# A transformer block on one core: from 128-row contractions and a planner to 64-row pairs and a written order

## The chip, the cores and the metric

The kernel runs on one core of a Trainium2 chip. The metric is the device time of one execution in microseconds (us); of the kernel before there are three timed runs, and their median is used.

## The reference

One block with adaptive layer norm: the vector `c` gives six modulation rows, the tokens go through a dilated sliding-window attention and then through an MLP. S = 2048 tokens, D = 448, 16 heads of 28, F = 1792, everything in bf16.

```python
mod = (_silu(c) @ w_mod).reshape(c.shape[0], 6, 1, -1)
sa, ca, ga, sb, cb, gb = ...
h = _layernorm(x) * (1 + ca) + sa
x = x + ga * _A_ref(h, A_wqkv, A_wo)
h = _layernorm(x) * (1 + cb) + sb
x = x + gb * _B_ref(h, B_w1, B_b1, B_w2, B_b2)

def _A_ref(x, wqkv, wo):          # 16 heads, window of 8 keys, every second token
    q, k, v = ...                 # x @ wqkv
    idx = pos[:, None] - 2 * jnp.arange(8)[None, :]
    logits = einsum('bhsd,bhswd->bhsw', q, k[idx]) * 28 ** -0.5   # masked where idx < 0
    o = einsum('bhsw,bhswd->bhsd', softmax(logits), v[idx])
    return o @ wo

def _B_ref(x, w1, b1, w2, b2):    # a second layer norm inside
    return gelu(_layernorm(x) @ w1 + b1) @ w2 + b2
```

A token attends to itself and to seven earlier tokens of its own parity, so even and odd tokens never meet in the attention.

## The kernel before

**Layout.** Even and odd tokens are two sequences of 1024, laid one behind the other along the free dimension. `x_all` holds 16 blocks of 128 tokens (eight of each parity). Transposed activations (`hT`, `qT`, `kT`, `oT`) have features or heads on the partitions and tokens along the free dimension. D = 448 is contracted in four steps of 128, 128, 128 and 64 or 65 rows (`KT`, `KW`, `KE`; the 65th row carries a bias or a zero), always on the whole array of TensorE (PE).

**Front.** `front_ln` takes the layer norm of two or four blocks (`stats`, `rstd_act` or `rstd_pool`, `normalize`), transposes on PE into `ptr` and applies scale and shift in `evac_h`. `front_qk` makes queries and keys, `pq`, with the weights spread to 32 rows per head by `spread`, in units of 256 (twice) and 512 (three times) columns: eight outputs m of four matmuls each, 160 matmuls in all. `mod_cols` makes the scale and shift columns from `silu_bf`; `mods` makes the other four modulation rows `pb`, stores them to `mod_hbm` and loads them back on all partitions (`mod_bc`). Behind that load, in the same SP queue, come the MLP weights (`load_mlp`).

**Attention.** Nine blocks, each of two sub-blocks of 114 queries in two windows. `values` copies the 64 key columns of two overlapping windows to `hw` and makes `pv` in four matmuls of 448 columns. `lmm` makes logits `lt` with keys on the partitions, in 32x64 tiles; ACT takes exp, DVE multiplies by `mask`. `dmm` makes the denominators `pd` with a matrix of ones and the outputs `po`, with heads on the partitions, in 64x32 tiles. ACT takes Ln and Exp of `pd` to get the reciprocals `lden`, and DVE's `div` multiplies into `oT`.

**After it.** `out_proj` makes `pw` from four head groups (`wo_s`, padded to 32 rows per head), adds it to `x_all`, takes both layer norms, and sends the result `ybuf` through a transposing DMA to `yT`. `x1p` on POOL keeps x plus the scaled bias of the MLP. `mlp` works on 256 tokens: per output tile of w1, four matmuls of 256 columns (`p1`), gelu on ACT into `hm`, then w2 with 14 matmuls of 448 columns per 128 tokens (`p2`), the residual on DVE and the store.

**Order.** Each piece is a task with an engine, an estimated time, reads, writes and buffers. `Planner.plan` runs a list schedule many times with perturbed ranks, keeps the best, and `emit` writes the program in that order, with filler matmuls (`pwm`) at the start. Each engine runs its instructions in the order written. PSUM has two large buffers (`L`, two banks) and four small ones (`S`, one bank).

The loop at the end of the kernel gives the phases: attention blocks 0 to 2, MLP tile 0; blocks 3 and 4, tiles 1 and 2; blocks 5 and 6, tiles 3 and 4; blocks 7 and 8, tiles 5 to 7.

Of the kernel before, what the change touches and what calls it, by code (L numbers as in the profile page):

```python
# [11 lines left out]
FP32 = mybir.dt.float32  # L12
# [5 lines left out]
DP = 512  # L18
KT, KR = 4, 64
KW = (128, 128, 128, KR)  # L20
KE = (128, 128, 128, KR + 1)
HP = 32
FT = F // 128
WIN = 8
SL = 1024
LEAD, SEP = 8, 8
WQ, WK, WE = 57, 64, 58
SBQ, NSB, NBT = 2 * WQ, 18, 9
SBE = 4 * WE
WT = LEAD + SL + SEP + SL + 4  # L30
OTW = NSB * SBQ
NBLK = S // 128
EPS = 1e-5
DEN_SCALE = 2.0 ** -32
EXP_SET = "natural_log_exp_and_others"
START, NOISE, WINDOW = 0.8, 0.02, 3.4133
SEED, TURNS = 44, 60
QKE = "AAADAAAD"
BONUS = (0.0, 0.0, 0.0)
SPREAD = (("DVE", "DVE"), ("DVE", "DVE"))  # L40
PHASES = [
    (range(0, 3), [0]),
    (range(3, 5), [1, 2]),
    (range(5, 7), [3, 4]),
    (range(7, 9), [5, 6, 7]),
]
LMM, DMM = 0.55, 0.80
FILL_UNTIL, FILL_SHARE = 12.0, 1.0
ROOM = {"L": 2, "S": 4, "et": 2, "den": 2, "zh": 6, "yT": 3, "hm": 3, "vb": 4, "hw": 3}
SWITCH, SAME = 0.095, 1.0  # L50
SEM = 0.07
DRAIN = {"PE": 0.165, "DVE": 0.085, "ACT": 0.105, "POOL": 0.05, "SP": 0.0}


class Buf:


    def __init__(self, room, make, name=""):
        self.room, self.make, self.name, self.users, self._t = room, make, name, [], None
        self.slot = None  # L60
# [8 lines left out]
class Task:  # L69
    def __init__(self, n, eng, us, fn, bufs, rank_add, late, dense, port, mode):  # L70
        self.n, self.eng, self.us, self.fn, self.bufs = n, eng, us, fn, bufs
        self.name = f"{eng} {fn.__qualname__.split('.')[-1]}:{fn.__code__.co_firstlineno}"
        self.rank_add, self.late, self.dense, self.port, self.mode = rank_add, late, dense, port, mode
        self.before, self.after = {}, []
        self.rank = 0.0
        self.fill = 0


class Planner:

    def __init__(self):
        self.tasks, self.writer, self.readers = [], {}, {}

    def add(self, eng, us, fn, reads=(), writes=(), bufs=(), after=(), order_after=(), rank_add=0.0, late=0.0, dense=1.0, port=False, mode="F"):
        t = Task(len(self.tasks), eng, us, fn, bufs, rank_add, late, dense, port or eng == "POOL", mode)
        for k in list(reads) + [b for b in bufs]:
            if k in self.writer:
                self._edge(self.writer[k], t, True)  # L90
        for k in writes:
            if k in self.writer:
                self._edge(self.writer[k], t, True)
            for r in self.readers.get(k, ()):
                self._edge(r, t, True)
            self.writer[k], self.readers[k] = t, []
        for k in reads:
            self.readers.setdefault(k, []).append(t)
        for b in bufs:
            b.users.append(t)  # L100
        for a in after:
            self._edge(a, t, True)
        for a in order_after:
            self._edge(a, t, False)
        self.tasks.append(t)
        return t

    def wrote(self, task, *bufs):
        for b in bufs:
            self.writer[b] = task  # L110

    def _edge(self, a, b, full):
        if a is b:
            return
        if a not in b.before:
            a.after.append(b)
            b.before[a] = full
        else:
            b.before[a] = b.before[a] or full

    def ranks(self):
        for t in reversed(self.tasks):
            tail = 0.0
            for a in t.after:
                lag = (DRAIN[t.eng] + SEM + t.late) if a.before[t] else 0.0
                tail = max(tail, a.rank + lag)
            t.rank = t.us + tail + t.rank_add

    def backward(self):

        used = {e: [] for e in DRAIN}
        for t in sorted(self.tasks, key=lambda t: (-(t.start + t.us), -t.n)):
            tail = 0.0
            for a in t.after:
                same = a.eng == t.eng and (t.eng == "PE" or not a.before[t])
                lag = 0.0 if same or not a.before[t] else DRAIN[t.eng] + SEM + t.late
                tail = max(tail, a.rank + lag)
            spans = used[t.eng]
            k = bisect.bisect_left(spans, (tail, 0.0))
            if k > 0 and spans[k - 1][1] > tail:  # L140
                tail = spans[k - 1][1]
            while k < len(spans) and spans[k][0] < tail + t.us - 1e-9:
                tail = max(tail, spans[k][1])
                k += 1
            t.rank = tail + t.us
            spans.insert(k, (tail, t.rank))

    def forward(self):
        left = {t: len(t.before) for t in self.tasks}
        ready_at = {t: 0.0 for t in self.tasks}  # L150
        ready = {e: [] for e in DRAIN}
        for t in self.tasks:
            if left[t] == 0:
                ready[t.eng].append(t)
        room = {r: [0.0] * n for r, n in ROOM.items()}
        users_left = {b: len(b.users) for t in self.tasks for b in t.bufs}
        free_at = {e: START for e in DRAIN}
        order = []
        now = START
        mode = "F"  # L160
        port = {"DVE": 0.0, "POOL": 0.0}
        while len(order) < len(self.tasks):
            started = False
            for e in ("PE", "DVE", "ACT", "POOL", "SP"):
                if free_at[e] > now:
                    continue
                best, best_key = None, None
                shared = e in port and port["DVE" if e == "POOL" else "POOL"] > now
                for t in ready[e]:
                    if ready_at[t] > now or (shared and t.port):  # L170
                        continue
                    key = (t.rank + (SAME if e == "PE" and t.mode == mode else 0.0), -t.n)
                    if best is not None and key < best_key:
                        continue
                    need = {}
                    for b in t.bufs:
                        if b.slot is None:
                            need[b.room] = need.get(b.room, 0) + 1
                    if all(sum(x <= now for x in room[r]) >= n for r, n in need.items()):
                        best, best_key = t, key  # L180
                if best is None:
                    continue
                t = best
                t.fill = 0
                if e == "PE" and now < FILL_UNTIL:
                    t.fill = int(max(0.0, now - free_at[e]) * FILL_SHARE / (0.43 if now < 6.8 else 0.215))
                ready[e].remove(t)
                order.append(t)
                t.start = now
                started = True  # L190
                for b in t.bufs:
                    if b.slot is None:
                        b.slot = min(range(ROOM[b.room]), key=lambda k: room[b.room][k])
                        room[b.room][b.slot] = 1e9
                end = now + t.us
                if e == "PE" and t.mode != mode:
                    end += SWITCH
                    mode = t.mode
                free_at[e] = end
                if t.port:  # L200
                    port[e] = end
                done = end + DRAIN[e] + t.late
                for b in t.bufs:
                    users_left[b] -= 1
                    if users_left[b] == 0:
                        room[b.room][b.slot] = done + SEM
                for a in t.after:
                    left[a] -= 1
                    at = done + SEM if a.before[t] else end
                    if a.eng == e == "PE" or (a.eng == e and not a.before[t]):  # L210
                        at = end
                    ready_at[a] = max(ready_at[a], at)
                    if left[a] == 0:
                        ready[a.eng].append(a)
            if started:
                continue
            times = [v for v in free_at.values() if v > now] + [v for r in room.values() for v in r if now < v < 1e9]
            times += [ready_at[t] for e in ready for t in ready[e] if ready_at[t] > now]
            if not times:
                return None, 1e9  # L220
            now = min(times)
        return order, max(t.start + t.us + t.late for t in self.tasks)

    def clear(self):
        for t in self.tasks:
# [755 lines left out]
```

## Time and profile before

| what | value |
|---|---|
| three timed runs | 186.35, 187.8, 188.04 us; median 187.8 us |
| span of the profiled execution, first to last instruction | 184.8 us |
| granted clock of TensorE, mean | 1.000 |
| DMA packets, bytes | 19,004, 13.99 MB |
| read from HBM, written | 9.70 MB, 1.84 MB |

The profile is one execution on its own; its time around the span is not shown, so the median stands 3.0 us above the span. "Busy" is the time in which an engine has an instruction in work; PE is the matmul, PEld the weight load that goes before each. The durations of single matmuls in the profile hold their latency as well, so the pace of a run of matmuls is read from the chain of waits, whose pieces follow one another without overlap. "Issue" in that chain is time in which the engine waited for nothing that the profile shows. A line like "L864" is the line of the kernel that issued the instruction.

### The profile page before, as it was taken

Reading aid. Unit: us, or ns where it says so; the run is one execution under the profiler, and the core shown is the slowest. Engines: PE = TensorE matmul, PEld = TensorE weight load, DVE = VectorE, ACT = ScalarE, POOL = GpSimd, SP = SyncE. Lnnn points to the kernel's source line nnn. Section 1 sums busy time; section 2 is a strip of 40 time slices with the busy share of each in tenths; the row PEclk is TensorE's granted clock in tenths of the full one; section 3 lists DMA queues with packets and bytes.
Section 4 is the critical chain, followed back from the end, with each engine's and each line's share of the span. In section 5 each row is a group of like instructions: output and inputs, shape, how many; then the busy total and the mean of one; then the engine's idle time right before and its main releaser. Section 6 shows DMA issues by size and latency. Waiting matters only on the chain.

```text
span 184.8 us, 5433 instructions
## 1 busy us (share of the span) xinstructions
PE 173.5 (94%) x2325; PEld 111.5 (60%) x2333; DVE 124.6 (67%) x348; ACT 103.8 (56%) x139; POOL 47.5 (26%) x97
## 2 busy tenths in 40 slices
PE   3997789899999999999999999999999999999991
PEld 0574565455458655775855567678556756857750
DVE  3799599889899799688424389693346968711102
ACT  2167667767486877766585667426786530521230
POOL 7074000508501602334200060532001526200000
PEclk9999999999999999999999999999999999999999
DMA  5999779900110101301210100213001012040101
GB/s 172 304 356 265 193 175 313 326 14 7 27 32 0 28 5 32 82 0 28 42 18 0 52 5 4 57 50 48 14 4 53 0 32 78 0 103 7 51 0 50
DMA packets 19004, 13.99 MB, mean 76 GB/s; under 512 B 9246, under 2 KB 18403, under 8 KB 18980
## 3 DMA queue, kind: packets, MB, share of 16 engines
q1 hardware_dynamic: 18978, 13.64, 27.7%
q8 instruction: 18, 0.29, 0.7%
q14 instruction: 6, 0.05, 0.1%
q10 hardware_dynamic: 2, 0.00, 0.0%
HBM read 9.70 MB, written 1.84 MB: 62 GB/s over the span
## 4 chain that ended last, share of the span: by engine, by line
PE 90%; DVE 4%; issue 2%; DMA 1%; ACT 1%; DVEq 0%
PE p L864 27%; PE p L885 23%; PE pq L640 13%; PE pv L708 7%; PE pw L814 7%; PE pwm L506 3%; PE lt L733 3%; PE po L773 3%; PE ptr L607 1%; PE pd L765 1%; DMA yT<-ybuf 1%; DVE st_all L513 1%; DVE kT L649 1%; ACT lden L788 1%; PE pb L661 0%
## 5 line engine op out<-in xcount | busy, mean ns | idle before, releaser
L864 PE MATMUL p<-yT,w_s 128*128 128x256 bf16 x448 | 52.3, 272 | 0.1
L871 ACT ACTIVATE hm<-p 128x1024 bf16<-128x1024 f32 (+1 forms) x32 | 28.8, 916 | 36.8 <-PE p L864 36.8
L864 PEld LDWEIGHTS <-w_s 128*128 128x128 bf16 x448 | 43.3, 97 | 8.9 <-issue 0.6
L885 PE MATMUL p<-w_s,hm 128*128 128x448 bf16 x224 | 46.9, 353 | 0.0
L531 POOL TENSOR_TENSOR rs_all<-tv_all,neg_half 128x1 f32<-128x1 f32 (+1 forms) x35 | 20.9, 605 | 52.3 <-DVE tv_all L528 47.5
L885 PEld LDWEIGHTS <-hm 128*128 128x128 bf16 x224 | 21.2, 98 | 17.9
L844 POOL TENSOR_TENSOR x1p_ring<-x_all,gbb_bc 128x448 f32<-128x448 bf16 x16 | 17.2, 1079 | 54.6 <-DVE x_all L818 45.3
L640 PE MATMUL pq<-hT,Wqk 128*128 128x512 bf16 (+3 forms) x153 | 30.0, 334 | 0.5 <-issue 0.2
L892 DVE TENSOR_TENSOR x_all<-p,x1p_ring 128x448 bf16<-128x448 f32 x16 | 9.8, 618 | 26.0 <-PE p L885 26.0
L640 PEld LDWEIGHTS <-Wqk 128*128 128x128 bf16 (+1 forms) x160 | 15.1, 97 | 11.5 <-DVE Wqk L626 0.2
L513 DVE BATCH_NORM_STATS2 st_all<-x_all 128x6 f32<-128x448 bf16 x32 | 19.1, 617 | 0.7 <-DMA x_all<-in_A_x_dram 0.5
L743 ACT ACTIVATE et<-lt 128x928 bf16<-128x928 f32 x18 | 16.0, 941 | 5.0 <-PE lt L733 4.9
L708 PE MATMUL pv<-Wv,hw 128*128 128x448 bf16 x72 | 16.4, 353 | 1.6 <-DVE hw L702 0.9
L751 DVE TENSOR_TENSOR et<-et,mask 128x928 bf16<-128x928 bf16 x18 | 11.7, 649 | 5.3 <-ACT et L743 5.3
L814 PE MATMUL pw<-wo_s,oT 128*128 128x448 bf16 x64 | 14.4, 352 | 0.0
L712 ACT CAST vbuf<-pv 128x448 bf16<-128x448 f32 x18 | 9.6, 532 | 6.3 <-PE pv L708 6.2
L818 DVE TENSOR_TENSOR x_all<-pw,x_all 128x448 bf16<-128x448 f32 x16 | 9.9, 620 | 4.4 <-PE pw L814 4.2
L785 ACT ACTIVATE lden<-pd 128x928 f32<-128x928 f32 x9 | 8.5, 948 | 7.1 <-PE pd L765 7.1
L652 ACT CAST kT<-pq 128x512 bf16<-128x512 f32 (+1 forms) x14 | 7.1, 510 | 8.6 <-PE pq L640 8.2
L708 PEld LDWEIGHTS <-hw 128*128 128x128 bf16 x72 | 6.7, 97 | 7.7 <-issue 1.2
L798 DVE TENSOR_TENSOR oT<-po,lden 128x456 bf16<-128x456 f32 x18 | 10.6, 623 | 0.6 <-ACT lden L788 0.6
L833 DVE BATCH_NORM_STATS2 st_all<-h 128x6 f32<-128x448 bf16 x16 | 9.8, 621 | 0.1
(83 smaller groups left out, 172.3 us busy)
## 6 DMA issues: line engine op xcount, KB each, us to landing
out_dram<-x_all SPq DMA_DIRECT2D x8, 224.0 KB, 2.0
w_s<-in_B_w_dram SPq DMA_DIRECT2D x2, 784.0 KB, 12.3
wmod<-in_w_mod_dram SPq DMA_DIRECT2D x2, 672.0 KB, 7.5
w_s<-in_B_w_dram SPq DMA_DIRECT2D x1, 1344.0 KB, 9.1
x_all<-in_A_x_dram SPq DMA_DIRECT2D x1, 896.0 KB, 7.9
wm_st<-in_w_mod_dram SPq DMA_DIRECT2D x1, 720.0 KB
wqk_st<-in_A_wqkv_dram SPq DMA_DIRECT2D x2, 339.0 KB, 5.7
x_all<-in_A_x_dram SPq DMA_DIRECT2D x2, 224.0 KB
```

The lines of the kernel that those rows point to most:

```text
L513: add("DVE", 0.53, lambda: nc.vector.bn_stats(out=st_all[:, sl, :], in_=src()), reads=key, writes=[f"st{sl}"])
L531: lambda: nc.gpsimd.tensor_tensor(out=rs_all[:, which, b0:b0 + n], in0=tv_all[:, which, b0:b0 + n], in1=neg_half[:, 0:n], op=ALU.pow),
L640: nc.tensor.matmul(pq.t[:], lhsT=wqk_m(kt, m), rhs=hT[0:KE[kt], kt, c0:c0 + n], start=(kt == 0), stop=(kt == KT - 1))
L708: nc.tensor.matmul(pv.t[:], lhsT=hw.t[0:KE[kt], kt].rearrange("p j k -> p (j k)"), rhs=Wv[0:KE[kt], kt, :], start=(kt == 0), stop=(kt == K ...
L743: ex = add("ACT", 0.825, lambda half=half: nc.scalar.activation(out=et.t[:, 2 * half:2 * half + 2].rearrange("p r n ft c -> p r (n ft c)") ...
L751: nc.vector.tensor_tensor(out=ev, in0=ev, in1=mask[:], op=ALU.mult)
L798: nc.vector.tensor_tensor(out=out, in0=pos[j].t[:], in1=rden.t[:, j, :, :, 0:WQ], op=ALU.mult)
L814: nc.tensor.matmul(pw.t[:], lhsT=oT[:, ft, c0:c0 + 128], rhs=wo_s[:, ft, :], start=(ft == 0), stop=(ft == 3))
L844: nc.gpsimd.tensor_tensor(out=x1p_ring[:, t % NX1P, :], in0=x_all[:, t, :], in1=gbb2_bc[:], op=ALU.add)
L864: nc.tensor.matmul(p1.t[:, f // 2, f % 2 * 256:f % 2 * 256 + 256], lhsT=w1_s[0:kp, kt, (fq + f) * 128:(fq + f + 1) * 128], rhs=yT.t[0:kp, ...
L871: gl = add("ACT", 0.18 + nf * 0.183, lambda fq=fq, nf=nf, p1=p1: nc.scalar.activation(out=hm.t[:, fq:fq + nf, :], in_=p1.t[:, 0:nf // 2, : ...
L885: nc.tensor.matmul(p2.t[:], lhsT=hm.t[:, ft, bi * 128:(bi + 1) * 128], rhs=w2_s[:, ft, :], start=(ft == 0), stop=(ft == FT - 1))
```

## The change

The kernel is written anew; the reference, the weights' use and the attention windows of 57 + 7 stay.

- **Layout.** Even tokens take partitions 0 to 63 and odd tokens 64 to 127: `hT`, `yT` and the weights hold D as seven steps of 64 rows (`KP`, `KS`), the weights on both halves. Each contraction is a pair of matmuls in two row tiles of 64, one for each parity, into two PSUM banks. `x_all` has 8 blocks of 128 positions, each with both parities side by side (896 columns).
- **Weights.** `load_both` issues seven DMAs per weight, each writing both halves; queries' and keys' weights stay unspread, and head groups of 28 columns are addressed in 32-column tiles. b1 is added by ACT in the gelu.
- **Queries and keys.** Per output m: 7 steps x 4 heads x 2 parities, in 64x32 tiles; units of 128, 128, 256 and 512 columns.
- **Attention.** Nine batches with both parities. Values in 64x64 tiles straight from `hT` (no `hw`). `pmm` has the queries on the partitions: the exponentials are the stationary operand, the values with a column of ones the moving one, so the denominators come out as a 29th column. DVE takes reciprocals and multiplies (`osb`), `omm` transposes back on PE, and a copy on ACT or DVE writes into `hT`, whose columns are free by then. Ln and Exp of the denominators go.
- **MLP.** Four tiles of 256 positions with both parities; w1 in pairs of 7 steps, w2 as before, whole-array.
- **PSUM.** Four buffers of two banks for everything.
- **Order.** A written list (`ORDER`, `SLOTS`) in place of the planner; phases: batches 0 to 4, tile 0; 5 and 6, tile 1; 7 and 8, tiles 2 and 3.

In the order of instructions PE has 4,668 rows before and 9,592 after (matmuls and weight loads), DVE 311 and 216, with repeated ones folded.

The core of the diff (task bookkeeping, constants and the lists left out):

```diff
-KT, KR = 4, 64
-KW = (128, 128, 128, KR)
-KE = (128, 128, 128, KR + 1)
+KP, KS = 7, 64
...
-PHASES = [
-    (range(0, 3), [0]),
-    (range(3, 5), [1, 2]),
-    (range(5, 7), [3, 4]),
-    (range(7, 9), [5, 6, 7]),
-]
+LN_UNITS = [[0], [1], [2, 3], [4, 5], [6, 7]]
+QK_UNITS = [[0], [1], [2, 3], [4, 5, 6, 7]]
+PHASES = [(range(0, 5), [0]), (range(5, 7), [1]), (range(7, 9), [2, 3])]
...
+    def load_both(dst, src, key):
...
+            for k in range(KP):
+                nc.sync.dma_start(out=dst[:, k], in_=bass.AP(src.tensor, src.offset + k * KS * row, [[0, 2], [row, KS], [1, n]]))
...
+    load_x(0, 1)
...
+    load_both(Wqkv[:, :, 0:D], A_wqkv[:, 0:D], "wq")
+    load_x(1, 2)
+    load_both(Wqkv[:, :, D:2 * D], A_wqkv[:, D:2 * D], "wk")
+    load_x(2, 4)
+    load_both(Wqkv[:, :, 2 * D:3 * D], A_wqkv[:, 2 * D:3 * D], "wv")
+    load_x(4, 8)
...
+    load_both(wo_s[:], A_wo, "wo")
...
-                for kt in range(KT):
-                    nc.tensor.matmul(pq.t[:], lhsT=wqk_m(kt, m), rhs=hT[0:KE[kt], kt, c0:c0 + n],
-                                     start=(kt == 0), stop=(kt == KT - 1))
+                for k in range(KP):
+                    for r in range(4):
+                        for s in range(NS):
+                            rows = slice(KS * s, KS * s + KS)
+                            w0, w = m * 4 * DH + r * DH, min(HP, top - HP * r)
+                            nc.tensor.matmul(pq.t[HP * r:HP * r + w, s, 0:n], lhsT=Wqkv[rows, k, w0:w0 + w],
+                                             rhs=hT[rows, k, c0:c0 + n], start=(k == 0), stop=(k == KP - 1),
+                                             tile_position=(KS * s, HP * r))
...
-            for kt in range(KT):
-                nc.tensor.matmul(pv.t[:], lhsT=hw.t[0:KE[kt], kt].rearrange("p j k -> p (j k)"), rhs=Wv[0:KE[kt], kt, :],
-                                 start=(kt == 0), stop=(kt == KT - 1))
+            for k in range(KP):
+                for j in range(2):
+                    for s in range(NS):
+                        rows = slice(KS * s, KS * s + KS)
+                        nc.tensor.matmul(pv.t[WK * j:WK * j + WK, s, 0:D], lhsT=hT[rows, k, kc + WQ * j:kc + WQ * j + WK],
+                                         rhs=Wqkv[rows, k, 2 * D:3 * D], start=(k == 0), stop=(k == KP - 1),
+                                         tile_position=(KS * s, WK * j))
...
+        def pmm():
...
+                            rows, col = slice(WK * j, WK * j + WK), j if s == 0 else 1 - j
+                            e0 = ((r * 2 + s) * 4 + ft) * WE
+                            nc.tensor.matmul(po.t[WK * col:WK * col + WK, s, HP * h:HP * h + DH + 1],
+                                             lhsT=et.t[rows, e0:e0 + WK], rhs=vb.t[rows, s, h, 0:DH + 1],
+                                             start=True, stop=True, tile_position=(WK * j, WK * col))
...
+        def omm():
...
+                        nc.tensor.matmul(pt.t[KS * s:KS * s + KS, j, k * WQ:k * WQ + WQ],
+                                         lhsT=osb.t[rows, s, k * KS:(k + 1) * KS], rhs=ident[rows, WK * col:WK * col + WQ],
+                                         start=True, stop=True, tile_position=(WK * col, KS * s))
...
+                    nc.tensor.matmul(pw.t[:, s, 0:D], lhsT=hT[rows, k, 128 * p:128 * p + 128], rhs=wo_s[rows, k, :],
+                                     start=(k == 0), stop=(k == KP - 1), tile_position=(KS * s, 0))
...
-                    for kt in range(KT):
-                        kp = KW[kt] + (kt == KT - 1)
-                        nc.tensor.matmul(p1.t[:, f // 2, f % 2 * 256:f % 2 * 256 + 256], lhsT=w1_s[0:kp, kt, (fq + f) * 128:(fq + f + 1) * 128],
-                                         rhs=yT.t[0:kp, kt, :], start=(kt == 0), stop=(kt == KT - 1))
+                    for k in range(KP):
+                        for s in range(NS):
+                            rows = slice(KS * s, KS * s + KS)
+                            nc.tensor.matmul(p1.t[:, s, 256 * fi:256 * fi + 256], lhsT=w1_s[rows, k, f * 128:(f + 1) * 128],
+                                             rhs=yT.t[rows, k, :], start=(k == 0), stop=(k == KP - 1),
+                                             tile_position=(KS * s, 0))
...
-    P.plan()
-    P.emit()
+    P.emit(filler)
```

## The prediction

> **What bounds the kernel now.** I read the page first, then the stages, then the chain of waits in order of time, then the timeline of TensorE (PE) around the places where that chain says "issue", and last the DMA view of single stretches. From the page, the span, the engines, the instruction queue and the chain by engine:
>
> ```profile
> span 184.8 us, 5433 instructions
> ...
> PE 173.5 (94%) x2325; PEld 111.5 (60%) x2333; DVE 124.6 (67%) x348; ACT 103.8 (56%) x139; POOL 47.5 (26%) x97
> ...
> q8 instruction: 18, 0.29, 0.7%
> ...
> PE 90%; DVE 4%; issue 2%; DMA 1%; ACT 1%; DVEq 0%
> ```
>
> TensorE carries 90% of the chain. Queue q8 fetched 18 packets for 4,658 PE instructions (2,325 matmuls, 2,333 weight loads): 0.29 MB / 18 = 16 KB, 259 instructions each. The stages (span, then busy time and count of each engine, clock, DMA share, GB/s):
>
> ```profile
> 0.00:10.50 10.50, 7.63 (x62) 3.63 (x64) 6.42 (x29) 2.98 (x6) 4.70 (x12) 1.00 0.85 251
> 10.50:54.00 43.50, 39.17 (x643) 23.12 (x644) 38.94 (x110) 29.96 (x52) 14.02 (x46) 1.00 0.62 171
> 54.00:180.60 126.60, 126.39 (x1624) 84.78 (x1628) 78.05 (x210) 70.88 (x82) 28.80 (x40) 1.00 0.13 29
> ```
>
> From 54.0 us on PE has no gap; before that it has some 9 us of them. Pieces of the chain (start, length, what), which give paces and not latencies:
>
> ```profile
> 19.53 1.29 issue
> ...
> 104.79 0.63 PE lt L733 x64
> 105.42 0.86 PE p L885 x4
> ...
> 108.55 0.32 PE pd L765 x8
> 108.87 0.55 PE po L773 x64
> ...
> 122.52 6.17 PE p L864 x56
> ```
>
> A 256-column matmul costs 0.110 (56 in 6.17), a 448-column one 0.189 (elsewhere in the chain 28 in 5.30, or four in 0.76), a matmul of the attention 0.0086 (64 in 0.55), one of the modulation columns 0.024 (32 in 0.78), a change of tile shape 0.10 (four w2 matmuls take 0.86 after lt, 0.76 elsewhere). The two pauses in po, on the timeline (start, length, what, idle before):
>
> ```profile
> 19.24 0.29 PE L773 MATMUL po<-et,vbuf 64*32 64x57 bf16 x22
> 20.82 0.49 PE L773 MATMUL po<-et,vbuf 64*32 64x57 bf16 x42 [1.29 <-issue]
> ...
> 34.29 0.71 PE L773 MATMUL po<-et,vbuf 64*32 64x57 bf16 x61
> 35.70 0.20 PE L773 MATMUL po<-et,vbuf 64*32 64x57 bf16 x3 [0.70 <-issue]
> ```
>
> Nothing in the data explains stopping inside one block of 64. Counted record by record, the pauses stand behind PE records 449 and 960, 511 apart: two fetch packets of 256. The DMA view has no q8 packet from 14.2 to 18.1 us and one from 18.1 to 19.7, and again none from 28.4 to 32.9 and one from 32.9 to 34.2:
>
> ```profile
> q1 hardware_dynamic: 351, 0.30, 107.7%
> q8 instruction: 1, 0.02, 5.6%
> ```
>
> So I read both pauses as PE out of instructions: it holds two blocks of 256, asks for the next when it enters the last one it holds, and the packet waits behind bulk loads. **Price of a block**, from entering the one before (about 64 records ahead of execution) to being usable: under bulk loads 27.6-28.4 to 35.70, and at most 10.6-14.2 to 20.82, so 7.4. Near the end of a load the packets began 1.15 and 1.04 after the pauses ended; with 1.2 for the packet and 1.2 from its end to the next instruction (19.61 to 20.82), 3.6. At rest there was no pause, so bounds: the start is 1.0-1.2 after entry, the packet lasts 0.9-1.45, and the rest lies between 0.2 (an ordinary transfer's last packet to its landing) and 1.55 (the second pause): 2.1 to 4.1; I take 3.0, the middle. At 256 instructions per 3.0 us, PE may use 85 per us. The old kernel uses 18 (w1) to 36 (256-column projections), and 205 only in bursts of 128 to 144.
>
> **The change on TensorE, if instructions are always there.** MLP up: 448 x 0.110 = 49.3 becomes 392 pairs x 0.110 = 43.1. MLP down: the same 224. Values: 72 x 0.189 = 13.6 becomes 63 groups of four, 11.9. Output projection: 64 x 0.189 = 12.1 becomes 56 pairs, 10.6. Query/key: 96 x 0.22 + 64 x 0.110 = 28.2 becomes 56 groups of eight 64x32 tiles per unit: two units of 128 columns at 8 x 0.0086 = 0.069 (issue, not width) 7.7, one of 256 at 0.110 6.2, one of 512 at 0.217 12.2, together 26.1. Attention: lt keeps its 576; pd and po, 9 x 0.87 = 7.8, become 576 + 252 matmuls x 0.0086 = 7.1; no row has two row tiles on one PSUM bank, as the new po and ot have them, so up to twice that, 14.2; I take 7.1, since at 29 and 57 columns issue is the nearer limit. [...] Transposes 64 to 56, -0.4; the modulation columns 32 to 112 at 0.024 each, +1.9, behind the load of their weights at first. Changes of tile shape, counted in the order of instructions: 39 become 54, +1.5. Sum: -6.2 - 1.7 - 1.5 - 2.1 - 0.7 - 0.4 + 1.9 + 1.5 = -9.2. That pairs overlap is borne out by pd: eight 464-column matmuls on two row halves in 0.32, where one after the other in two rows would take 0.39.
>
> **The other engines** stay under PE. ACT loses Ln and Exp of the denominators (8.5 + 9.6) and gains 9 copies of 798 elements (about 0.85 each), about -10. DVE loses hw, the spreading and the 18 divisions (5.4 + 1.8 + 10.6) and gains 9 reciprocals and 9 multiplications of 896 elements (1.09, from 0.425 at 256 and 0.692 at 512), so near 121. The doubled weights cost 3.2 MB and 42 DMA issues of 0.5 us on SP where 14 were. Early loads are then 7.4 MB: at 283 GB/s (2 to 23 us now) until 28 us, SP's 36 issues until 18, hidden by the data. What stands behind on SP is the store and broadcast of the modulation, and then w1 and w2, 5.3 MB: 18.9 us at 279 GB/s, issued 4.5 after the modulation matmuls (19.10 to 23.57 now). The eight transposing DMAs (1.2 issue, 2.4 landing) are each far ahead of their w1.
>
> **What the change adds in instructions.** PE's stream grows from 4,668 to 9,592, and the growth sits early: query/key has 1,792 matmuls for 160. With places in the new stream: query/key from 322, modulation at 2,396, the 256-column unit to 3,580, the 512-column one 4,542 to 5,566, first w1 at 5,834. At its own pace, 322 to 4,542 takes 33 us: 128 instructions per us against 85.
>
> Walk by blocks. Records 0 to 447 are there at the start. Block 448 is asked for at about 8.0 (the modulation columns): 15.4. 704, under loads: 22.8. 960, near their end: 26.4. Five more at 3.0: 2,240 at 41.4, so the modulation at 42.5 (18.2 now) and w1/w2 loading from 47.0 to 65.9. 2,752 at 47.4; 3,008 and 3,264 under loads, 54.8 and 62.2; 3,520 near their end, 65.8. To 4,542 four blocks, 12.0: 77.8. The 512-column unit runs at its own pace, 12.9, since a block lasts 16 x 0.217 = 3.5: 90.7. To the first w1 3.4: 94.1 (54.0 now). From there the prices above give 104.3: PE ends at 198.4. The tail stays 4.2 (180.6 to 184.8): span 202.6. The span of 184.8 stands 3.0 under the median of 187.8, which I add: **206**. With 2.1 at rest on the eleven blocks and 6.6 under loads it is 193, with 4.1 and 8.1 throughout 230.
>
> **Rivals.**
> - *Instructions never limit PE*, the pauses being an accident of the start. For: two pauses in 18 bursts. Then 180.6 - 9.2 + 4.2 + 3.0 = 178.6, faster. It decides if a block costs under 2.1 at rest and 3.6 under loads; break-even is about there. Against: the pauses' distance and the packets' times. [...] Chance 0.16.
> - *Fetch partly hidden* (blocks ahead, or 2.1 and 5): 188 to 193. Chance 0.08.
> - *The clock falls.* PE would be busy 1.1 of every 3 us or 7.4 us; no row shows that, and the clock is 1.00 in all stages. With half the clock as a bound that I assume, the 512-column unit doubles, +12: 218. [...] Chance 0.16.
> - *Pairs don't overlap*, so the change doesn't do what it says: w1 +43, output +11, values +12, query/key +26: about 298. Against: pd and lt. Chance 0.03.
>
> **Numbers.** The forecast has 0.57, its own range 193 to 226. 186 to 226 takes in the second and third rivals and leaves out the first and last. About 1% is what a measurement here can tell from no change. Faster by more: 0.17; within: 0.04 (both with what the second rival gives to them, 0.01 and 0.04); slower: 0.79, the rest.
>
> **What would show it.** About 37 q8 packets; PE idle with "issue" at every 256 records in query/key, some 40 us in all; the modulation matmuls beyond 40 us; first w1 at 85 to 105 and after it 105 us without gaps; w1 at 1.54 per 14 pairs, values at 1.33 per 28. A first w1 before 65 us, or query/key of 128 columns at 3.9 per unit without pauses, makes the forecast wrong.

## The result, and the profile after

The changed kernel takes 284.36 us (median of four runs, 284.07 to 284.52), the one before 187.78 beside it (186.35 to 188.04): a ratio of 1.517, interval 1.511 to 1.522. It is slower, as forecast, but by 97 us where the forecast had 18, and 58 us beyond the end of its range. Ratios are taken over fast runs alone: the run of experiment 1 that was profiled, 239.28 us, was a slow one, 1% above the median of its other three.

From the page of the changed kernel: the span, the engines, PE and its clock by fortieths of the span (7.06 us each), the DMA share, the instruction queue, the chain by engine, and what query/key on PE waited for (after the last bar, idle time before it and what ended most of it).

```profile
span 282.3 us, 10267 instructions
...
PE 185.2 (66%) x4795; PEld 122.2 (43%) x4795; DVE 121.4 (43%) x275; ACT 100.6 (36%) x149; POOL 38.7 (14%) x67
...
PE   7823216223586677796000009999999999999995
...
PEclk9675555555579599999555557999999999999999
DMA  5111131186112111111115512010130310013001
...
q8 instruction: 37, 0.61, 0.9%
...
PE 42%; SPq 39%; DMA 10%; issue 3%; DVE 3%; ACT 1%
...
L437 PE MATMUL pq<-hT,Wqkv 64*32 64x128 bf16 (+5 forms) x1792 | 38.1, 329 | 38.0 <-DMA Wqkv<-in_A_wqkv_dram 21.3
```

PE's share of the chain fell from 90% to 42%, and SPq, the engine that issues the loads, took 39% where before it had none to speak of. The 37 instruction packets are the forecast's number. The clock, 1.00 in every stage before, reads 5 tenths in ten of the first twenty slices. Of the idle time ahead of query/key, 21.3 us ended with the landing of its weights. The stages (stretch, its length, busy time and count of PE, PEld, DVE, ACT, POOL, clock, DMA share, GB/s):

```profile
0.00:52.00 52.00, 23.68 (x692) 13.82 (x693) 12.03 (x39) 8.74 (x20) 4.93 (x29) 0.62 0.24 73
52.00:62.70 10.70, 2.21 (x16) 0.41 (x12) 1.74 (x5) 0.26 (x1) 0.70 (x1) 0.50 0.56 161
62.70:90.00 27.30, 16.09 (x799) 11.87 (x799) 12.72 (x36) 8.89 (x16) 2.05 (x3) 0.67 0.31 83
90.00:174.30 84.30, 38.82 (x1418) 25.02 (x1419) 32.06 (x66) 26.36 (x36) 10.27 (x10) 0.74 0.23 70
174.30:279.20 104.90, 104.45 (x1878) 71.09 (x1874) 62.27 (x132) 56.34 (x78) 20.79 (x24) 1.00 0.13 30
```

The last stage begins with the first w1 and PE is busy in all but 0.45 us of it; it lasts 104.9 us. Everything that was lost lies before it: 174.3 us where the kernel before took 54.0. (Five attention batches of nine now stand there instead of three, one reason why the last stage is shorter than the 126.6 us before.) What SP did at the start (start, length, line, what, how many):

```profile
1.72 16.01 SPq L235 DMA_DIRECT2D Wqkv<-in_A_wqkv_dram  x7
17.78 2.23 SPq L240 DMA_DIRECT2D x_all<-in_A_x_dram  x1
20.06 15.58 SPq L235 DMA_DIRECT2D Wqkv<-in_A_wqkv_dram  x7
35.68 2.51 SPq L240 DMA_DIRECT2D x_all<-in_A_x_dram  x1
38.23 16.25 SPq L235 DMA_DIRECT2D Wqkv<-in_A_wqkv_dram  x7
```

Each of these DMAs of `load_both` holds SP for 2.2 to 2.3 us on average; most of those before took 0.4 to 0.6. Two of the kernel before, for the same weights:

```profile
2.44 0.58 SPq L387 DMA_DIRECT2D wqk_st<-in_A_wqkv_dram  x1
3.07 0.49 SPq L390 DMA_DIRECT2D wqk_st<-in_A_wqkv_dram  x1
```

In the changed kernel a transfer of `x_all` on an ordinary pattern between them takes as long (2.23 and 2.51 us); I read that as standing behind what is queued. The chain from the modulation on (start, length, what):

```profile
85.15 4.48 DMA mod_hbm<-mod_rows
89.63 0.02 issue
89.65 0.35 SPq L469
...
91.25 4.17 SPq L235
95.41 0.04 issue
95.45 4.41 SPq L235
99.86 0.04 issue
99.91 4.43 SPq L235
...
150.87 13.75 DMA w_s<-in_B_w_dram
164.62 0.02 issue
164.65 0.62 DVE w_s L482
```

w1's fourteen DMAs of 224 KB stand one behind another, most of them 4.4 to 4.5 us each (the longest 5.97, all together 56.28), until 146.3, w2 behind them, and the last weights land at 164.6. What moved meanwhile, from the DMA view of 91 to 146 us (queue, packets, MB, share of 16 engines):

```profile
DMA packets 1606, 3.16 MB, mean 57 GB/s; under 512 B 38, under 2 KB 1492, under 8 KB 1594
...
q1 hardware_dynamic: 1594, 2.97, 14.3%
```

A share of 14.3% is little more than two of sixteen engines, 12.5%. So the first reading was: each DMA whose source begins with `[0, 2]` runs on two engines, and SP stands until there is room behind it. That such a DMA writes both halves of the partitions is not it: w2's two DMAs in the same kernel write all 128 partitions too, from a source with 128 rows outermost, and from 151 to 160 us the queue's share is 75.9%.

### The profile page after: what moved, and what is told of

Its sections match the earlier page's. It is cut to its first block, busy times and chain, and to the rows that moved or that the text cites. A ratio compares the mean times of both kernels' runs of the same rounds, so it can differ in the third digit from the quotient of the medians.

```text
span 282.3 us, 10267 instructions
## 1 busy us (share of the span) xinstructions
PE 185.2 (66%) x4795; PEld 122.2 (43%) x4795; DVE 121.4 (43%) x275; ACT 100.6 (36%) x149; POOL 38.7 (14%) x67
## 4 chain that ended last, share of the span: by engine, by line
PE 42%; SPq 39%; DMA 10%; issue 3%; DVE 3%; ACT 1%
SPq L235 35%; PE p L673 15%; PE p L654 15%; DMA w_s<-in_B_w_dram 5%; DMA Wqkv<-in_A_wqkv_dram 4%; PE pv L512 3%; PE pw L602 3%; PE pq L437 2%; SPq L240 2%; DMA mod_hbm<-mod_rows 2%; SPq L266 2%; PE lt L533 1%; PE po L560 1%; DVE osb L570 1%; PE pt L582 1%
## 5 line engine op out<-in xcount | busy, mean ns | idle before, releaser
L437 PE MATMUL pq<-hT,Wqkv 64*32 64x128 bf16 (+5 forms) x1792 | 38.1, 329 | 38.0 <-DMA Wqkv<-in_A_wqkv_dram 21.3
L437 PEld LDWEIGHTS <-Wqkv 64*32 64x32 bf16 (+1 forms) x1792 | 26.7, 110 | 49.1 <-DMA Wqkv<-in_A_wqkv_dram 23.6
L662 ACT ACTIVATE hm<-p,b_col 128x512 bf16<-128x512 f32 x56 | 35.3, 684 | 25.4 <-PE p L654 25.1
L654 PE MATMUL p<-yT,w_s 64*128 64x256 bf16 x784 | 44.1, 269 | 0.0
L377 POOL TENSOR_TENSOR rs_all<-tv_all,neg_half 128x2 f32<-128x2 f32 x22 | 15.8, 726 | 179.7 <-DVE tv_all L375 137.7
L654 PEld LDWEIGHTS <-w_s 64*128 64x128 bf16 x784 | 37.8, 94 | 5.7 <-issue 0.4
L673 PEld LDWEIGHTS <-hm 128*128 128x128 bf16 x224 | 21.3, 98 | 19.7 <-ACT hm L662 0.2
L361 DVE BATCH_NORM_STATS2 stt<-x_all 128x6 f32<-128x448 bf16 x32 | 18.5, 613 | 25.7 <-DMA x_all<-in_A_x_dram 25.6
L512 PE MATMUL pv<-Wqkv,hT 64*64 64x448 bf16 x252 | 18.6, 425 | 10.5 <-DMA Wqkv<-in_A_wqkv_dram 10.1
L638 POOL TENSOR_TENSOR Wqkv<-x_all,gbb_bc 128x448 f32<-128x448 bf16 x16 | 17.1, 1087 | 33.0 <-DVE x_all L683 18.1
L602 PE MATMUL pw<-wo_s,hT 64*128 64x448 bf16 x112 | 12.1, 350 | 2.0 <-issue 1.2
```

Source lines behind the costliest of these rows:

```text
L361: add("DVE", 0.53, lambda: nc.vector.bn_stats(out=stt[:, w, b, :], in_=src()), reads=reads, bufs=bufs, writes=[f"st{w}_{b}"], name="stats")
L377: add("POOL", 0.42 + 0.15 * n, lambda: nc.gpsimd.tensor_tensor(out=r, in0=tv, in1=neg_half[:, 0:n], op=ALU.pow), reads=[f"tv{w}_{b0}", "ne ...
L437: nc.tensor.matmul(pq.t[HP * r:HP * r + w, s, 0:n], lhsT=Wqkv[rows, k, w0:w0 + w], rhs=hT[rows, k, c0:c0 + n], start=(k == 0), stop=(k == ...
L512: nc.tensor.matmul(pv.t[WK * j:WK * j + WK, s, 0:D], lhsT=hT[rows, k, kc + WQ * j:kc + WQ * j + WK], rhs=Wqkv[rows, k, 2 * D:3 * D], start ...
L602: nc.tensor.matmul(pw.t[:, s, 0:D], lhsT=hT[rows, k, 128 * p:128 * p + 128], rhs=wo_s[rows, k, :], start=(k == 0), stop=(k == KP - 1), til ...
L638: add("POOL", 1.0, lambda n=n: nc.gpsimd.tensor_tensor(out=x1p.t[:, n, :], in0=xn(p, n), in1=gbb2_bc[:], op=ALU.add), reads=[f"x{p}", "gbb ...
```

## The experiments

Theory A: the pattern of `load_both` puts each DMA on two of sixteen engines. Rival B: SP pays for the number of DMAs, whatever their pattern. Theory C, the forecast's own: PE is short of instructions in query/key, hidden so far under the loads; once they are quick it shows. Rival to C: instructions never limit PE.

**1. Two DMAs per weight, 64 rows outermost.** Bytes and destinations stay.

```diff
-            for k in range(KP):
-                nc.sync.dma_start(out=dst[:, k], in_=bass.AP(src.tensor, src.offset + k * KS * row, [[0, 2], [row, KS], [1, n]]))
+            for h in range(NS):
+                nc.sync.dma_start(out=dst[KS * h:KS * h + KS], in_=src.rearrange("(k p) n -> p k n", p=KS))
```

> The doubled weights come with two DMAs per weight, one per half of the partitions, 64 rows each as the slowest dimension, instead of seven whose source has 2 as its slowest dimension; bytes and all else are the same. Theory A (a DMA whose slowest source dimension is 2 moves on two of the 16 engines, and SP stands behind it): DMA share near 1.0 up to 25-30 us instead of 0.1-0.2, no SP issue over 1 us, modulation matmuls at 40-50 us instead of 79. Theory C (besides, PE runs out of instructions, 3.45 us per 256): 200 to 215 us, with pauses named issue about every 256 records in query/key. Rival, loads alone: 177 to 183 us and no such pauses. Theory B (SP pays 2.5 us per DMA of this kind whatever its shape): faster as well, as there are fewer DMAs, but DMA share stays under 0.3.

Measured: 237.13 us (234.65 to 239.28), 1.264 of before (1.255 to 1.272). 47 us come back, and the DMA share in the loads is 0.99, but 200 to 215 was expected; the modulation matmuls come at 60.6 instead of 40 to 50, and behind the loads SP still stands 4.74 us for one DMA (`b_rows`) and 7.82 us for one of w2; stages of this kernel, columns as above, up to its first w1:

```profile
0.00:31.00 31.00, 16.10 (x479) 9.30 (x480) 9.86 (x30) 4.48 (x11) 4.20 (x28) 0.72 0.99 215
31.00:64.00 33.00, 19.90 (x863) 14.05 (x863) 11.26 (x37) 11.01 (x23) 1.61 (x3) 0.59 0.17 32
64.00:88.00 24.00, 9.87 (x417) 8.05 (x417) 7.20 (x17) 5.14 (x8) 3.56 (x5) 0.66 0.98 213
```

The DMA share is 0.99 and 0.98 in the two loads, at 215 and 213 GB/s. Between them, from 31 to 64 us, almost nothing is loaded, and PE is busy 19.9 of 33 us. Its chain in query/key shows why (start, length, what):

```profile
14.24 0.65 PE pq L437 x62
14.89 3.35 issue
18.25 1.91 PE pq L437 x111
20.15 5.94 issue
26.09 1.91 PE pq L437 x111
28.00 6.76 issue
34.76 1.91 PE pq L437 x111
```

Bursts and pauses in turn. The 1.91 us are 128 matmuls with their 128 weight loads (some records are missing), that is one block of 256, and 5.94 and 6.76 us of pause behind one such burst make 7.9 and 8.7 us per block under the loads. The whole chain has 19% of "issue", some 46 us. What follows: A holds and is worth 47 of the 97 us, and C holds too, larger than forecast: with the loads mended 50 us over before remain, not the gain that the rival to C gives.

**2. Fourteen DMAs per weight, 64 rows outermost.** One per half and step: `[[row, KS], [1, n]]` in place of `[[0, 2], [row, KS], [1, n]]`, twice as many DMAs as in the change.

> Fourteen DMAs per doubled weight, one per half and step of 64 rows: twice as many DMAs as in the changed kernel, the same bytes, 64 as the slowest dimension. Theory A: about 0.5 us of SP each, so 56 early ones take 28 us; the time is within 10 us of the kernel with two DMAs per weight. Theory B (a cost per DMA, not per shape): 84 DMAs at 2.5 us or more, so slower than the changed kernel, over 290 us.

Measured: 228.0 us (one run). Twice the DMAs, and SP pays 0.84 us for each (0.5 was expected) instead of 2.3; the first fourteen on this kernel's SP timeline:

```profile
1.73 11.78 SPq L236 DMA_DIRECT2D Wqkv<-in_A_wqkv_dram  x14
```

So it is not the number: B falls. That it is quicker than experiment 1 was not taken apart; its loads are spread over a longer time (49.6% of the queue from 4 to 30 us), and its chain has 10% of "issue" where that of experiment 1 has 19%.

**3. The stride of zero.** In the changed kernel the outermost entry reads two different steps of 64 rows, so that half the weights are those of another step.

```diff
-                nc.sync.dma_start(out=dst[:, k], in_=bass.AP(src.tensor, src.offset + k * KS * row, [[0, 2], [row, KS], [1, n]]))
+                nc.sync.dma_start(out=dst[:, k], in_=bass.AP(src.tensor, src.offset + (k if k < 5 else k - 2) * KS * row, [[2 * KS * row, 2], [row, KS], [1, n]]))
```

> The changed kernel, with one number of load_both changed: the outermost entry of the source, which repeats the same 64 rows for the other half (two times stride zero), gets a stride of two steps, so that the halves read two different steps of 64 rows. Half of the weights are then those of another step, and the outputs are other numbers; shapes, sizes and the count of instructions stay. If it is the count of 2 on the outside that puts each DMA on two engines: DMA share near 0.13 to 0.16 while w1 loads, SP standing 2.5 us per small and 4.5 us per w1 DMA, and 280 to 288 us as in the changed kernel. If it is the stride of zero, or both halves reading the same addresses: SP under 1 us per DMA, DMA share above 0.6 in the loads, and 228 to 240 us.

Measured: 284.85 us (one run). SP again stands 16.29 and 15.60 us for seven DMAs, and in the load of w1 the queue's share is about the same (14.3% in the changed kernel):

```profile
q1 hardware_dynamic: 1512, 2.69, 13.3%
```

So neither the stride of zero nor two reads of one address matters; two as the outermost count does: the queue's share is 13.3 and 14.3% with 2, and the DMA share is 0.99 with 64 (experiment 1, 0 to 31 us). What other counts give, no run shows.

**4. and 5. Each half of the loads alone.** Experiment 1 for the weights of the attention only, and for w1 only.

> Two DMAs per weight for queries, keys, values and output projection; w1 keeps its 14 DMAs with 2 as the slowest dimension. Theory A: modulation at 55-60 us as with all loads mended, then 14 x 4.5 us on SP and the w2 load behind them, so the first w1 at 140 to 155 us and the time 252 to 268 us. If the early loads were the whole delay: 240 us or less.

> The other half: two DMAs per w1 half, the weights of queries, keys, values and output projection with seven DMAs as in the changed kernel. Theory A: modulation at about 80 us as in the changed kernel, w1 and w2 landed some 22 us later, first w1 at 115 to 135 us, time 225 to 247 us. If the w1 load did not matter: 275 us or more.

Measured: 259.49 and 260.35 us (one run each), so 24.9 and 24.0 of the 47.2 us. The first is as expected (first w1 at 149.0). The second is a miss: the modulation came at 82.4 as expected, but the first w1 at 149.9 instead of 115 to 135. Between the two the chain runs over PE and DVE and no longer over the loads, with pauses of 6.13, 5.95 and 2.89 us, which the slow loads had covered; 11% of the whole chain is "issue".

**6. Query/key in pairs.** To test C with the loads mended: the weights are spread to 32 columns per head in SBUF (POOL clears the padding, DVE, ACT and POOL copy), and one matmul over 128 columns takes the place of four over 32. PE's rows fall from 9,592 to 6,904, at the same widths.

```diff
-                    for r in range(4):
-                        for s in range(NS):
...
-                            nc.tensor.matmul(pq.t[HP * r:HP * r + w, s, 0:n], lhsT=Wqkv[rows, k, w0:w0 + w],
...
+                    for s in range(NS):
+                        rows = slice(KS * s, KS * s + KS)
+                        nc.tensor.matmul(pq.t[:, s, 0:n], lhsT=wide["t"][rows, k, m * 128:(m + 1) * 128],
+                                         rhs=hT[rows, k, c0:c0 + n], start=(k == 0), stop=(k == KP - 1),
+                                         tile_position=(KS * s, 0))
```

> Two DMAs per weight as in the first, and queries and keys in pairs of 64x128 tiles with weights spread to 32 columns per head (DVE, ACT and POOL copy once), so 448 matmuls instead of 1792; PE rows fall from 9592 to 6904, the columns streamed stay the same. Theory C: 10.5 blocks of 256 fewer; query/key takes its own 25 us instead of 14 blocks x 3.45 = 48, so 15 to 25 us faster than the first kernel, 180 to 192 us. Rival, loads alone: within 3 us of the first kernel.

Measured: 208.05 us (206.41 to 208.22), 1.113 of before (1.109 to 1.118): 29 us less than experiment 1, where 15 to 25 were expected, though not the 180 to 192 that were, since experiment 1 itself came out higher. From its page:

```profile
span 204.7 us, 7555 instructions
...
PEclk9859769699785579999999999999999999999998
...
q8 instruction: 27, 0.44, 1.0%
...
PE 68%; DVE 10%; DMA 9%; issue 7%; SPq 2%; POOL 1%; ACT 1%; POOLq 0%
```

Ten packets fewer, "issue" from 19% to 7% (14.5 us), and the clock reads 0.77 to 0.86 in the stages ahead of w1 (experiment 1: 0.59 to 0.91), so the 29 us hold what the higher clock gives as well (28 `pv` take 2.76 us at 5 tenths, from 56.27 us in experiment 1, and 1.45 at 1.00, from 137.74). The first w1 starts at 96.3 instead of 129.2, and what follows it still takes 105 us. This kernel is 21 us over the one before; its chain ahead of w1 shows the keys' weights landing at 18.2 and POOL's copy of them until 21.2, four pauses of 2.5 to 5.2 named "issue", a stretch of DVE work from 76 to 92, and 4.55 for a `yT` transfer. These were not tested one by one.

**7. The same, with the slow loads.** Experiment 6 with `load_both` as in the change.

> Only the wide query/key tiles, with the seven DMAs per weight left as in the changed kernel. Theory A: the loads set the first w1 at 174 us whatever PE does before, so 275 to 287 us. If the instructions were the main cause: 255 us or less.

Measured: 283.82 us (one run). Of the 29 us nothing is left, for the loads cover the pauses.

```profile
SPq 51%; PE 38%; DMA 7%; DVE 2%; issue 1%
```

**8. All copies of the transposed tokens on DVE.** In experiment 6's chain ACT and DVE wait on one another copy by copy (0.57 and 0.42 us in turn). All seven on DVE:

```diff
+            eng = "" if t.name == "evac_h" else eng
```

> The kernel with two DMAs per weight and wide query/key tiles, and the seven scale-and-shift copies of each transposed unit all on DVE, where ACT and DVE took turns. In the trace the two engines wait for one another copy by copy (0.34 and 0.46 us, starts 0.87 apart per pair). Theory D (two engines on one transposed buffer run one after the other, so the second engine brings nothing): the seven copies of a 128-column unit take 7 x 0.34 = 2.4 instead of 2.9 us, those of 256 columns 7 x 0.35 = 2.5 instead of 3.5; the time falls by 1 to 5 us. Rival (they overlap, and DVE is the scarcer engine): slower by 1 to 5 us.

Measured: 207.81 us (206.70 to 209.60), 1.110 (1.101 to 1.119): the same as experiment 6, a miss. Seven copies of 256 columns do take 2.4 us instead of 3.3, but the end does not move.

**9. The kernel before, with narrow query/key.** The reverse test of C: `pq` in four column tiles of 32, 960 more rows on PE (4,668 to 5,628), in another tile shape; all else stays.

```diff
-                    nc.tensor.matmul(pq.t[:], lhsT=wqk_m(kt, m), rhs=hT[0:KE[kt], kt, c0:c0 + n],
-                                     start=(kt == 0), stop=(kt == KT - 1))
+                    for r in range(4):
+                        nc.tensor.matmul(pq.t[HP * r:HP * r + HP, :], lhsT=Wqk[0:KE[kt], kt, m // 4, m % 4 * 4 + r, :],
+                                         rhs=hT[0:KE[kt], kt, c0:c0 + n], start=(kt == 0), stop=(kt == KT - 1),
+                                         tile_position=(0, HP * r))
```

> The kernel before, with each query/key matmul of 128 columns of weights cut into four of 32 columns in four column tiles: 640 instead of 160, the same columns streamed, loads and all else as before. PE rows rise from 4668 to 5628. Theory C (a block of 256 costs 3.5 to 4.2 us at rest and 8 to 9.5 under loads, so PE is held at 61 to 73 rows per us at rest and 27 to 32 under loads; query/key would take 37 with 512 columns and 73 with 256): more pauses at every 256 records in the first 50 us, 22 packets instead of 18, slower by 4 to 14 us, of which the changes of tile shape explain 2 to 4 (0.10 each). Rival (the instructions cost nothing, the pauses were an accident): 2 to 4 us slower from the tile shapes alone, with no more than two pauses.

Measured: 194.46 us (193.82 to 195.88), 1.037 of before (1.030 to 1.044), 6.8 us more. 30 more changes of tile shape at the prediction's 0.10 are 3.0 of them; the pauses of 0.3 us and more in the chain of the front go from 2.0 to 4.1 us. The other 1.7 were not taken apart. In its chain:

```profile
14.73 0.31 PE lt L735 x26
15.04 2.87 issue
17.91 0.32 PE lt L735 x30
```

The pause stands inside a block of logits that waits for no data, at PE record 448: the first block boundary, as in the kernel before, only 4.5 us earlier, since query/key uses up the instructions sooner.

## Why the prediction was wrong in size and right in direction

**The step that failed** is the loads: "42 DMA issues of 0.5 us on SP where 14 were", the early ones "until 18, hidden by the data", at 283 GB/s until 28 us. I took the price of an issue from DMAs of another pattern, though `[[0, 2], [row, KS], [1, n]]` stood in the diff and no row before had a source with an outermost count of two. Of the early weights' 28 DMAs the first 21 took 2.2 to 2.3 us each on average, the last seven 3.4, so SP's early issues lasted until 85.0 instead of 18; w1's 14 took 4.0 on average. The modulation matmuls came at 81.3 instead of 42.5, the last weights of the MLP landed 83.3 behind them instead of 23.4, and the first w1 came at 174.3 instead of 94.1. Experiments 1 to 3 show the cause, a DMA pattern with two as outermost count, and it is worth 47 us with everything else as changed. The forecast missed by 78 us; the other 31, from 206 to the 237 of experiment 1, lie in the price of instructions, below, and in what stays unresolved there.

**Right:** PE's work and the pairs. From the first w1 on 104.9 us against 104.3; 112 matmuls of w1 in 6.11, so 0.109 per pair against 0.110, and the rival in which pairs do not overlap falls. Part of that stretch (start, length, what):

```profile
174.29 6.11 PE p L654 x112
180.41 0.61 PE po L560 x64
181.02 1.64 PE p L654 x28
182.66 1.45 PE pv L512 x28
184.10 0.22 PE pt L582 x28
```

64 `po` take 0.61 with the change of shape, 128 take 1.17 elsewhere, against 0.55 per 64. The prediction's other end, 14.2, would make it twice that; the trace does not agree, though the new `po` has two row tiles on one bank. The tail is 3.1 us instead of 4.2. The 3.0 us added to the span are 1.8 here (284.07 against 282.3), as in the kernel before, where a run of 186.55 has the span of 184.8: the median had been set against the span of a quicker run.

**Right in kind, too small:** instructions by blocks. The changed kernel's pauses stand behind PE records 705, 1217, 1729, 1985 and on in steps of 256, each ending 1.3 to 1.7 us after the end of a packet, which agrees with the two-block reading of the kernel before. The prices were low. In the changed kernel one packet mostly follows the other by 3.4 to 4.0 us at rest, and in experiment 1 one block of query/key starts 4.0 us after the other at rest (3.0 in the sum, 4.1 its upper end) and 7.8 to 9.5 under loads (7.4). The pauses of experiment 1 come at record 449 and in steps of 256 after it. The loads themselves run at 213 to 215 GB/s even when mended, not 280.

With these, the prediction's walk for experiment 1 (8.4 per block under the loads, 3.8 at rest, the loads at 4 to 31 and 64 to 88) has block 960 at 33.2, block 2,240 at 52.2, 3,008 at 63.6, 3,776 at 88.8, the 512-column unit from 100.2, and the first w1 at 116.5. Measured: 129.2. Some 13 us of that front are thus not resolved. Experiments 6 and 9 say that the number of instructions costs, by taking them away (29 us, a higher clock with it) and by adding them (6.8 us, of which 2.1 in pauses and 3.0 by the price of tile shapes); with the pauses at steps of 256 records, each just behind a packet, the rival in which they never limit falls.

**The clock** was a rival at 0.16, as one price of 12 us. It did fall, to 0.50 from 52.0 to 62.7 us, where PE mostly waited, and to 5 tenths in most slices before 70 us; in experiment 1 it is 0.59 between the loads. There 128 matmuls of 128 columns take 1.91 us (1.10 at the prediction's 0.0086), still less than a block's 3.4, so the fetch, not the clock, sets the pace of those units. For the 256-column unit two blocks took 3.61 and 3.62 in experiment 1, where 16 groups of eight at 0.110 give 1.76 and the block before took 1.94; but pauses of 5.87 and 3.40 follow them, so under the loads PE waited for instructions there too. What the lower clock cost besides, no run separates.

## What to carry to other kernels

Read the outermost count of a DMA's source pattern before pricing it: an outermost count of two cost 47 us here, by stalling the issuing queue and everything behind it. And count instructions where many small ones follow one another: a form with a quarter of the matmuls gave 29 us at the same widths. The two costs lie one over the other, so the second mend shows its worth only with the first done: the pairs gave nothing with the slow loads and 29 us without them. (The halves of the loads, 24 and 25 us, stand one behind the other and nearly add up to the 47 of both.)

## What the runs showed of the hardware

- While DMAs with two as outermost count ran, 57 GB/s were moved (the changed kernel, 91 to 146 us) and 53 (experiment 3, 92 to 146 us), and one held SP 2.3 us per 112 KB and mostly 4.48 us per 224 KB, as did other transfers queued behind them (2.23 and 2.51 us). With 64 it was 213 to 215 GB/s in experiment 1, 0.7 us of SP per 392 KB at first and more later in the loads (3.3 us for one of `wo_s`), and 0.74 to 0.84 us per 56 KB in experiment 2. The stride of zero makes no difference (284.85 against 284.36 us).
- A block of 256 PE instructions costs 3.4 to 4.0 us with the DMA engines mostly idle (packet to packet in the changed kernel, block to block in experiment 1) and 7.8 to 9.5 while they are at 0.98 to 0.99 (experiment 1), some twice as much.
- The clock reads 5 tenths where PE works in bursts of 1.9 us with pauses of 2 to 7 us between them (experiment 1, 18 to 41 us), and 1.00 where PE is busy 104.45 of 104.90 us (the changed kernel from 174.3 us on).
